# An offset for each step's key in a planner: the same steps in another order, in a linear attention with a two-layer FFN on one Trainium2 core

## The chip, the cores and the metric

The kernel runs on one core of a Trainium2 chip. The metric is device time in microseconds (us) of one execution: 371.3 us in the median of three runs of the kernel before (371.17 to 372.02). The engines are TensorE (PE, whose weight loads are shown apart as PEld), VectorE (DVE), ScalarE (ACT), GpSimd (POOL) and SyncE (SP); 16 DMA engines move data. All three runs agree within 0.3%.

## The reference

`q`, `k` and `v` have 8 batches of 8 heads with 576 tokens of 64 numbers. The attention has no softmax over pairs of tokens: each token gets 256 features, and a head's 576 keys are summed up in one 256 x 64 matrix. Behind it stands a feed-forward network (FFN) over all 4608 tokens, in which the heads of a token lie side by side as 512 numbers.

```
def phi(x):
    proj = np.einsum('bhsd,df->bhsf', x, w_phi)                  # 64 -> 128
    proj = proj - np.max(np.abs(proj), axis=-1, keepdims=True)
    return np.concatenate([np.exp(proj), np.exp(-proj)], axis=-1)
q_p, k_p = (phi(q), phi(k))
kv = np.einsum('bhsf,bhsd->bhfd', k_p, v)
z = np.sum(k_p, axis=2)
num = np.einsum('bhsf,bhfd->bhsd', q_p, kv)
den = np.einsum('bhsf,bhf->bhs', q_p, z)[..., None] + 1e-06
attn = num / den
...
h = np.maximum(x @ w_in, 0.0)          # 4608 x 512 by 512 x 2048
out = h * h @ w_out                    # 2048 -> 512
```

## The kernel before

**Steps.** The kernel doesn't issue instructions as it goes. It first records *steps* (`Op`), each a few instructions on one engine, then lets a planner put them in an order, and then emits them in that order. The recording passes over the batches (loads, `k_batch`, `q_batch`) and then over the FFN's chunks of tokens (`hp_chunk`, `op_chunk`). These are the steps, with the lines that the profile shows:

- Loads of `k`, `q`, `v` by POOL's DMA queue (L379 for 512 tokens of each head, L387 for the other 64, called "rest"); `w_in` in two halves (L406) and `w_out` in two halves (L411), all to bf16. One batch's `q`, `k` and `v` have two buffers each.
- Transposes of `k` and `q`: on PE for batches 0 and 1 (L508, L686, with an identity), by a transposing DMA of SP's queue from batch 2 on (L436, L440).
- Key features: `kp` (L537) projects, in five groups for each batch, with matmuls that use 64 rows of PE's array; DVE takes the largest absolute value (L475), ACT the two exponentials (L482), and `em` (L562) the exponentials of the largest values. The factors that belong to the subtraction of the maximum are multiplied to `v` (`va`, L604 and L594, on POOL, for batch 0 on POOL or DVE).
- `kv` (L621, L626): PE sums keys by values, with a column for `z`; ACT or DVE copies the result (L449, L451).
- Query features: `qm` (L708) and `qp` (L717), again on 64 rows, with a DVE maximum (L745) and two ACT exponentials (L739) and `e2` (L753).
- `nd` (L769; L777 for the rest tokens, where it uses 64 columns of the array): numerator and denominator; DVE adds the two halves (L797, L801), takes the reciprocal (L818) and multiplies (L825), which gives `xo`, 128 tokens of FFN input.
- The transpose of `xo` to `xT`: on PE for batches 0 and 1 (L860), by SP's DMA from batch 2 on (L844, L847).
- FFN, first product `hp` (L899): four chunks of 128 tokens, then sixteen of 256. Each chunk of 256 has eight hp steps of 8 matmuls with 256 columns; a chunk of 128 has four of 16 matmuls with 128 columns. ACT or DVE takes the ReLU (L914, L916), DVE squares it (L923).
- FFN, second product `op` (L945): for 128 tokens four steps of 4 matmuls with 512 columns, with the same PSUM buffer; then a copy (L449, L451) and a store by SP's queue (L969, L966).

**Buffers.** PSUM has two rings: `pj`, three buffers, for everything of the attention, and `mo`, two buffers, for the transposes on PE and for hp and op. A step that needs a buffer waits until the step that reads the last owner is done. Other rings are in SBUF: five for `xT`, two for the squared `h`, four for the ReLU's result.

**Keys and order.** Each step is recorded by `add` with a key, in microseconds: roughly when it is due. An FFN step's key comes from a list with a pitch of 1.2 us, in which hp steps of one chunk alternate with op steps of the chunk before. A step of the attention has a key some microseconds ahead of the chunk that will need it. `order` simulates the engines with fixed costs for each step. In each round it takes the engine whose earliest possible step starts soonest, and among the steps that can start there within a short window (`WINDOW`, 0.15 us on PE, 0.1 on ACT and DVE) it takes the one with the smallest key plus a penalty for starting later:

```
near = [c for c in can if c[2] == e0 and c[0] <= soon + self.WINDOW[e0]]
...
t, o, e = min(near, key=lambda c: c[1].key + self.BETA * (c[0] - soon))
```

Where a step may run on either of two engines, the planner takes the one on which it would be done sooner. The order that comes out, in time of the planner's simulation, is the order of every engine's instructions and of every DMA queue. Steps are numbered in the order of their recording; a DMA takes two numbers, one for its issue and one for its transfer.

Of the kernel before, what the change touches and what calls it, by code (L numbers as in the profile page):

```python
# [11 lines left out]
ALU = mybir.AluOpType  # L12
ACT = mybir.ActivationFunctionType
INF = float("inf")


class Slots:
# [8 lines left out]
    def take(self):  # L26
        n = self.free.index(min(self.free))
        self.free[n] = INF
        return n
# [48 lines left out]
class Plan:  # L78
# [21 lines left out]
        return o, d  # L100

    def add(self, key, engines, emit=None, deps=(), take=(), give=(), after=(), locks=(), port=False, mode="full"):
        op = Op(key, engines, emit, deps, take, give, after, locks, port, mode)
        self.ops.append(op)
        return op

    def order(self):
# [8 lines left out]
        def start(o, e):  # L116
# [12 lines left out]
            if o.ring:  # L129
                ring = rings.setdefault(o.ring[0], [])  # L130
                for n in range(len(ring) - self.DEPTH, len(ring) - self.DEPTH + o.ring[1]):
                    if n >= 0:
                        t = max(t, ring[n].seen or INF)
            if o.port and e in ("dve", "pool"):
# [5 lines left out]
        while ready:  # L140
            can = [(start(o, e), o, e) for o in ready for e in o.engines]
            soon, _, e0 = min(can, key=lambda c: c[0])
            if soon == INF:
                raise RuntimeError("; ".join(sorted(f"{o.emit.__qualname__} {o.key:.1f}" for o in ready if o.emit)))
# [64 lines left out]
def kernel(  # L209
# [154 lines left out]

    o_wst, d_wst = plan.issue("hw", 2, -99, {"sp": (1.2, 1.2)}, c_wst, 0.1)
    o_var = add(-99, {"dve": (1.9, 1.9)}, c_var)
    o_w2 = add(-98, {"dve": (0.6, 0.7)}, c_w2, [d_wst], after=[o_var])
    o_ready = add(-200, {"pool": (1.2, 1.2)})
    srcs = {"k": k, "q": q, "v": v}
    tiles, loads = {}, {}  # L370
# [648 lines left out]
```

## Time and profile before

| | before |
|---|---|
| runs shown, median (lowest to highest) | 371.3 us (371.17 to 372.02) |
| profiled execution | 370.85 us |
| its span, first to last instruction | 369.0 us |
| granted TensorE clock, mean | 0.998 |
| idle before the first transposes on PE, for k and for q | 6.6 us, 4.1 us |
| first hp matmul (L899) starts | 30.3 us |
| last op matmuls (L945) end | 365.0 us |

The profile is of one execution. Busy time is the time in which an engine had an instruction under way; a matmul's end is modelled, so that a busy PE may still lose time between matmuls. In the lists of waits a row gives the engine and line that waited, what it waited for, the sum in us, how often, and the longest. "Issue" there means that the profile shows nothing that the engine waited for. In the chain that ended last a row gives start, length and what ran.

The chain of the whole program is PE for 70% (L899 28%, L945 27%), then DVE 9% and DMA 8%. Loads fill the start: w_in's halves land at 22.1 and 27.7 us, batch 1's keys at 30.1, w_out's at 35.6 and 40.6, and the DMA engines are busy in nearly all of the first 110 us.

### The profile page before, as it was taken

What the parts mean: (1) busy time and instruction counts of PE and PEld (TensorE: products, weight loads), DVE (VectorE), ACT (ScalarE), POOL (GpSimd) and SP (SyncE); (2) the same over time, 40 slices, a digit from 0 to 9 for tenths busy, and PEclk for the clock granted to TensorE, in tenths of its full rate; (3) what the DMA queues carried; (4) which work ended last, traced back from release to release, by engine and by line L of the source; (5) the groups of instructions that cost most, each with busy time, mean ns of one, the idle gap of its engine ahead of it and who ended that gap; (6) DMA issues with size and microseconds to landing.
All of it is one profiled execution on the core that took longest, in us unless ns stands there. A gap on an engine that the chain in (4) does not pass through costs nothing.

```text
span 369.0 us, 9166 instructions
## 1 busy us (share of the span) xinstructions
PE 338.3 (92%) x3788; PEld 235.5 (64%) x3836; DVE 271.0 (73%) x463; ACT 239.6 (65%) x376; POOL 139.3 (38%) x181
## 2 busy tenths in 40 slices
PE   2378989899999999999899999999999999999995
PEld 2267756766686667477576756676677666767662
DVE  4979787999777678878756899679469896857220
ACT  2855677869577864477854898379648954654441
POOL 8644138966930069302390029200920191000000
PEclk9999999999999999999999999999999999999999
DMA  7999999999994272974918154762113102211112
GB/s 83 182 207 204 200 204 152 172 200 180 120 187 75 58 157 42 177 121 94 157 45 117 50 122 66 106 125 74 25 45 62 44 2 60 71 45 47 40 38 78
DMA packets 90009, 39.07 MB, mean 106 GB/s; under 512 B 57584, under 2 KB 84336, under 8 KB 89968
## 3 DMA queue, kind: packets, MB, share of 16 engines
q0 software_dynamic: 41168, 18.36, 40.2%
q1 hardware_dynamic: 48800, 20.13, 26.6%
q8 instruction: 30, 0.49, 0.5%
q14 instruction: 11, 0.09, 0.1%
HBM read 36.77 MB, written 9.44 MB: 125 GB/s over the span
## 4 chain that ended last, share of the span: by engine, by line
PE 70%; DVE 9%; DMA 8%; ACT 4%; issue 3%; POOL 3%; SPq 2%; DVEq 0%; ACTq 0%; POOLq 0%
PE mo L899 28%; PE mo L945 27%; DMA xT<-xo 5%; PE pj L626 4%; PE pj L769 3%; DVE m L475 3%; DMA vin<-in_v_dram 2%; ACT kph L482 2%; PE pj L708 2%; DVE h L923 2%; PE pj L717 1%; SPq L847 1%; PE pj L621 1%; PE pj L537 1%; DVE hr L916 1%
## 5 line engine op out<-in xcount | busy, mean ns | idle before, releaser
L899 PE MATMUL mo<-xT,win 128*128 128x256 bf16 (+1 forms) x1280 | 144.1, 262 | 3.5 <-DMA xT<-xo 1.9
L945 PE MATMUL mo<-wout,h 128*128 128x512 bf16 x528 | 135.4, 379 | 4.1 <-issue 1.0
L899 PEld LDWEIGHTS <-win 128*128 128x128 bf16 x1280 | 111.7, 98 | 31.3 <-issue 6.3
L914 ACT ACTIVATE hr<-mo 128x512 bf16<-128x512 f32 x113 | 67.7, 601 | 60.0 <-PE mo L899 55.9
L923 DVE TENSOR_TENSOR h<-hr 128x512 bf16<-128x512 bf16 x144 | 71.9, 509 | 34.3 <-ACT hr L914 33.9
L945 PEld LDWEIGHTS <-h 128*128 128x128 bf16 x576 | 52.9, 98 | 48.4 <-issue 2.6
L739 ACT ACTIVATE qph<-pj 128x1024 bf16<-128x1024 f32 (+1 forms) x80 | 71.6, 945 | 16.5 <-PE pj L717 16.3
L482 ACT ACTIVATE kph<-pj 128x1024 bf16<-128x1024 f32 (+1 forms) x80 | 71.2, 954 | 10.8 <-PE pj L537 7.6
L604 POOL TENSOR_TENSOR va<-vin,em 128x512 bf16<-128x512 bf16 x57 | 61.4, 1111 | 0.6
L745 DVE TENSOR_REDUCE mq<-pj 128x8 f32<-128x1024 f32 (+1 forms) x40 | 44.4, 1109 | 10.9 <-PE pj L708 10.1
L475 DVE TENSOR_REDUCE m<-pj 128x8 f32<-128x1024 f32 (+1 forms) x40 | 43.8, 1108 | 2.4 <-PE pj L537 2.2
L573 POOL CAST va<-em 128x64 bf16<-128x64 f32 (+1 forms) x11 | 4.9, 446 | 104.5 <-ACT em L562 104.5
L797 DVE TENSOR_TENSOR tmp<-pj,e 128x520 f32<-128x520 f32 x32 | 22.1, 691 | 15.4 <-PE pj L769 14.8
L825 DVE TENSOR_TENSOR xo<-tmp,rden 128x512 bf16<-128x512 f32 (+1 forms) x40 | 29.4, 736 | 0.3
L449 ACT ACTIVATE ot<-mo 128x512 f32<-128x512 f32 x30 | 18.0, 599 | 17.2 <-PE mo L945 13.4
L801 DVE TENSOR_TENSOR tmp<-pj,tmp 128x520 f32<-128x520 f32 x32 | 22.2, 695 | 6.1 <-PE pj L769 5.8
L769 PEld LDWEIGHTS <-qph 128*128 128x128 bf16 x512 | 20.6, 98 | 5.5 <-issue 1.0
L916 DVE TENSOR_SCALAR hr<-mo 128x512 bf16<-128x512 f32 x31 | 21.0, 683 | 3.8 <-PE mo L899 3.7
L626 PE MATMUL pj<-va,kph 128*128 128x65 bf16 x512 | 23.4, 200 | 0.0
L626 PEld LDWEIGHTS <-kph 128*128 128x128 bf16 x512 | 22.3, 102 | 1.1
L769 PE MATMUL pj<-kvs,qph 128*128 128x65 bf16 x512 | 22.4, 194 | 0.4 <-ACT kvs L449 0.4
L449 ACT ACTIVATE kvs<-pj 128x520 bf16<-128x520 f32 x15 | 9.1, 604 | 15.1 <-PE pj L626 15.1
(55 smaller groups left out, 244.4 us busy)
## 6 DMA issues: line engine op xcount, KB each, us to landing
out_dram<-ot SPq DMA_DIRECT2D x32, 256.0 KB, 2.4
vin<-in_v_dram POOLq DMA_DIRECT2D x8, 512.0 KB, 9.7
qin<-in_q_dram POOLq DMA_DIRECT2D x8, 512.0 KB, 9.2
kin<-in_k_dram POOLq DMA_DIRECT2D x7, 512.0 KB, 11.7
win<-in_moe_w_in_dram POOLq DMA_DIRECT2D x2, 1024.0 KB, 14.9
wout<-in_moe_w_out_dram POOLq DMA_DIRECT2D x2, 1024.0 KB, 19.3
out_dram<-ot SPq DMA_DIRECT2D x8, 128.0 KB, 2.3
xT<-xo SPq DMA_TRANSPOSE x36, 2.6
```

Source lines behind the costliest of these rows:

```text
L475: nc.vector.tensor_reduce(out=st["m"].rearrange("p (n c) -> p c n", c=2)[:, :, n0 : n0 + n], in_=st["pj", g][:, :, :n], axis=AX.X, op=ALU. ...
L482: nc.scalar.activation(out=st["kph"][:, s, n0 : n0 + n].rearrange("p n c f -> p c n f"), in_=st["pj", g][:, :, :n], func=ACT.Exp, scale=1. ...
L604: eng.tensor_tensor(out=st["va"][:, s, gs, 0:D], in0=tiles["v", b].rearrange("p h i d -> p (h i) d")[:, gs, :], in1=st["em"][:, s, gs].uns ...
L626: nc.tensor.matmul(out=kv[:, sum_of(h), :], lhsT=st["kph"][:, s, 2 * h + i // 2, i % 2, :], rhs=st["va"][:, s, h * NI + i, :], start=False ...
L739: nc.scalar.activation(out=st["qph", pt][:, s, :, n0 : n0 + n], in_=st["pq", pt, gi][:, :, :n], func=ACT.Exp, scale=1.0 - 2.0 * s)
L745: nc.vector.tensor_reduce(out=st["mq", pt][:, :, n0 : n0 + n], in_=st["pm", pt, gi][:, :, :n], axis=AX.X, op=ALU.max, apply_absolute_value ...
L769: nc.tensor.matmul(out=nps[:, sl, :], lhsT=qph[:, s, half, sl, :], rhs=kvs[:, s, sum_of(sl), :], start=True, stop=True)
L825: nc.vector.tensor_tensor(out=xo[:, :nh], in0=st["tmp", pt, half][:, :nh, 0:D], in1=st["rden", pt, half][:, :nh].unsqueeze(2).to_broadcast ...
L899: nc.tensor.matmul(out=hp[:, mi, :], lhsT=win[:, kc, mc * P : (mc + 1) * P], rhs=st_x[c][:, kc, 0:nt, :], start=(kc == 0), stop=(kc == KC1 ...
L914: nc.scalar.activation(out=out_, in_=in_, func=ACT.Relu)
L923: eng.tensor_tensor(out=st["h2"][:, mcs[0] : mcs[-1] + 1, 0 : nt * P], in0=hr, in1=hr, op=ALU.mult)
L945: nc.tensor.matmul(out=st["op"].rearrange("p a b -> p (a b)"), lhsT=hst["h2"][:, mc, tt * P : (tt + 1) * P], rhs=wout[:, mc, :], start=(mc ...
```

## The change

A table `SHIFT` has one whole number for each step in the order of recording, from -50 to 50; `add` adds half of it, so at most 25 us, to the step's key. Nothing else differs: the same steps are recorded with the same costs, buffers, engines to choose from and dependencies, and the planner is the same. The numbers were found by a search that ran without a chip. Since keys decide the order, and the order decides where a step with two possible engines goes, the order of instructions changes on all engines and on both DMA queues, and so does the engine of a few steps.

```
+SHIFT = (
+    -13, 0, -23, 5, -19, -5, 0, -11, 26, 0, -13, 0, -5, 0, -28, 0, -5, 0, -10, 0, -3, 0, -37, 0, 0, 0,
...
+    -2, 0, 4, -26, -17, -4, 0, 18, 0,
+)
...
     def add(self, key, engines, emit=None, deps=(), take=(), give=(), after=(), locks=(), port=False, mode="full"):
+        key += 0.5 * SHIFT[len(self.ops)]
         op = Op(key, engines, emit, deps, take, give, after, locks, port, mode)
```

## The prediction

> **What bounds the kernel now.** First the page's busy shares and the windows of 18.45 us: they show where TensorE, the busiest engine, loses time.
>
> ```profile
> PE 338.3 (92%) x3788; PEld 235.5 (64%) x3836; DVE 271.0 (73%) x463; ACT 239.6 (65%) x376; POOL 139.3 (38%) x181
> ...
> 0.00:18.45 18.45, 5.88 (x62) 4.22 (x62) 13.28 (x20) 10.80 (x19) 13.87 (x25) 1.00 1.04 132
> 18.45:36.90 18.45, 14.85 (x241) 12.72 (x243) 15.22 (x26) 10.49 (x17) 8.28 (x13) 1.00 1.25 206
> 36.90:55.35 18.45, 16.27 (x216) 11.98 (x219) 14.73 (x26) 13.17 (x21) 4.68 (x8) 1.00 1.46 202
> 55.35:73.80 18.45, 16.61 (x282) 12.47 (x285) 15.61 (x29) 14.43 (x24) 17.31 (x23) 1.00 1.30 162
> 73.80:92.25 18.45, 17.33 (x189) 11.60 (x187) 18.40 (x32) 14.96 (x24) 11.80 (x17) 1.00 1.51 190
> ...
> 239.85:258.30 18.45, 18.24 (x193) 12.63 (x194) 15.84 (x25) 15.72 (x24) 0.00 (x0) 1.00 0.47 100
> ```
>
> A row gives the stretch, then busy time of PE, PEld, DVE, ACT and POOL, then clock and DMA. From about 110 us PE is busy 98-99% of a window; before that it is not, and DVE is what is full (18.40 of 18.45). So there are two stages with two limits.
>
> To see what PE really loses I price its steps by their fastest rows in the chain of waits:
>
> ```profile
> 355.51 0.86 PE mo L945 x4
> 356.38 0.87 PE mo L899 x8
> ```
>
> With these and the like (one 8-matmul step at L769 0.24, one kv step at L621/L626 1.34) PE's whole program is 321.8 us of work. Following the trace's weight loads in program order, the step that comes after PE's 35th us of it starts at 62.1 us, after the 60th at 92.4, after the 85th at 118.1. Lost by then (start less the work done): 26.8, 31.6, 33.1. The last step stands at 43 lost. So 33 is gone by 118 us, only 10 after.
>
> The early part is DVE's. In program order, by waits direct and through other engines, I count how much DVE work must be finished before PE may start a step (DVE instructions priced by their group rows). "Lead" is that less the PE work already done: before PE's 35th us 10.9, its 60th 15.3, its 85th 10.8. DVE's idle time, from the windows, adds up to 5.2, 8.4, 12.1, 15.0, 15.0 at the ends of the first five. At 92 us lead plus idle is 15.3 + 15.0 = 30.3 against 31.6 lost; at 74 us (PE work 45) 12.7 + 15.0 = 27.7 against 28.7. That sum, plus about 1.2 us of latency, is what PE has lost: DVE sets the end of this stage.
>
> The late part: what PE and its weight loads wait for from 110 to 365 us.
>
> ```profile
> PEld L708 <- issue: 7.2, 21, 0.4
> PEld L899 <- issue: 3.9, 18, 0.3
> PEld L537 <- issue: 2.7, 9, 0.4
> PEld L777 <- issue: 1.7, 6, 0.4
> PEld L945 <- issue: 1.5, 7, 0.3
> ...
> PE mo L899 <- DMA xT<-xo: 1.9, 3, 0.9
> PE mo L945 <- issue: 0.6, 4, 0.2
> PE mo L899 <- ACT hr L914: 0.3, 1, 0.3
> ```
>
> PE waits for almost nothing (2.8 us). But weight loads stand idle, with no releaser, where a step on half of the array (L537, L708, 64 rows; L777, 64 columns) follows a whole-array step, and where a whole-array step follows it.
>
> **The change, part by part.** It removes no work: TensorE has the same matmuls, the same DMAs are issued. Three ReLU evictions go from DVE (0.683) to ACT (0.601), two kvs copies go from ACT and one va product from POOL to DVE, ten small copies swap between DVE and ACT: by the group rows DVE's sum rises by 1.1 us, ACT's falls by 1.0, POOL's by 1.1, none on the late path. What changes is the order, on every engine. PE's neighbours of different kind fall from 405 to 334: hp steps and op steps (the two FFN products) now stand in longer runs.
>
> 1. *Start.* The load queue of POOL keeps k0, v0, q0, w_in, k1, w_out, q1; only k2 goes ahead of v1. The first FFN step stands after 8.4 instead of 7.8 us of PE work and needs 21.4 instead of 21.0 us of DVE work; a transpose of k1 now stands just before it, and k1 landed at 30.1, the old first step began at 30.30. Nothing changes that DVE doesn't hide: 0.
>
> 2. *DVE's stage.* The new order asks more of DVE sooner: lead 15.3 at PE's 15th us (before 10.4), 17.0 at the 35th (10.9), 14.0 at the 60th (15.3), 15.3 at the 85th (10.8). More backlog should leave DVE less idle. These are its waits from 20 to 95 us before:
>
> ```profile
> DVE tmp L797 <- PE pj L769: 2.4, 1, 2.4
> DVE hr L916 <- PE mo L899: 1.9, 2, 1.1
> DVE m L475 <- PE pj L537: 1.6, 1, 1.6
> ```
>
> All are for PE steps that the order may bring sooner. Idle until 36.9 us (8.4) is the loads' and stays. Of the 6.6 us after it, I let half go, being unable to see more without a run: 11.7. PE has then lost 17.0 + 11.7 + 1.2 = 29.9 at its 35th us (more than the 26.8 of before) and, as the lead doesn't rise again, still 29.9 at its 85th, against 33.1: -3.2. Bounds: all 6.6 gone, 26.6, -6.5; none gone, 33.2, +0.1.
>
> 3. *Changes of array form.* After 80 us of PE work the order had 40 entries into half-array steps and 36 returns from 64-row steps; now 34 and 29. By the rows an entry costs (7.2 + 2.7 + 1.7) / 36 = 0.32, a return (3.9 + 1.5) / 25 = 0.22; spread over all 40 and 36, 0.29 and 0.15. So 6 x 0.29 + 7 x 0.15 = -2.8; at the full row price -3.4; if weight loads catch up inside the next step, 0. PE is full there, so I take -2.8.
>
> 4. *Other PE waits late.* 0.9 us besides DMA; covers between a step and the eviction it needs are longer in the new order (more PE work stands between). -0.5, from -0.9 to +0.5.
>
> 5. *Transposes by DMA* (L844, L847), which bring the FFN's input. PE work between the last PE step that a chunk's transposes need and the chunk's first step (its last one) was, in order of chunks, 8.5, 7.4, 9.2, 7.5, 8.0, 6.4, 8.3 up to PE's 185th us; now 6.6, 8.6, 6.4, 6.8, 7.4, 9.8, 6.6. The chain and the tile's view price it:
>
> ```profile
> 107.25 6.97 DMA xT<-xo
> ...
> 150.24 6.77 DMA xT<-xo
> ...
> DMA to landing us min/median/max: 2.3/2.6/7.7
> ```
>
> A clean landing takes 2.4; while q, v and k of a later batch are in flight (issued 98.7 to 106.0 and 144.1 to 152.8) it took 7. With 2.3 of DVE (0.69 + 0.70 + 0.20 + 0.74) and 1.2 of issue, clean is 5.9, inside every cover; met by loads 10.5, 3.8 beyond a cover of 6.7. The first load burst stands behind batch 2's products of V, which now wait for 67.1 us of DVE work (71.1 before), and the transpose that met it for 92.2 (89.8): 6.4 us further apart, against 7.7 of overlap. The next burst starts 6 us of PE work sooner. One may meet, one that met is freed: 0, from -1.9 (the waits above gone) to +3.8 (one more met).
>
> 6. *DVE beside POOL.* L923 takes 0.424 in the median and up to 1.259; in 55.3 to 92.2 us, thirteen took 7.98, 2.4 more than thirteen medians. Which of them stand beside POOL's products the order doesn't tell: 0, from -2.4 to +2.4. (The Trainium skill, SBUF — State Buffer, Who interferes with whom: a DVE instruction with two SBUF inputs and a GpSimd one that reads SBUF block each other for a whole instruction. The long ones agree. It speaks against a DVE that has less idle time while POOL works: by it the meetings would double, +2.4 in the sum, 367.2.)
>
> The last step, its copy and store stay: 32 matmuls of L945 at the end in the new order too.
>
> **Sum.** -3.2 - 2.8 - 0.5 = -6.5. The profiled execution took 370.85 us (span 369.0, 1.85 around it), so 364.35; the median of the runs is 0.45 above it: 364.8.
>
> **Rivals.**
> *DVE's stage gives nothing.* Idle stays 15.0, as its waits are for latency and not for backlog; for it: lead 17.0 comes as early as the 35th us. Against: more released work stands in front of DVE. -2.8 - 0.5: 368.0.
> *DVE never idles after the loads.* For it: lead never below 13.6 from PE's 10th to its 50th us. Against: three of its waits are for PE steps behind 2 us of chain. -6.5 - 3.4 - 0.5 - 0.5 (half of the DMA waits and more): 360.4.
> *Transposes meet loads (slower).* Place: the first step of the chunks with covers of 6.4 to 6.9 (five of them, three before). Price 3.8 each. It decides from two on: 7.6 - 6.5, 372.4; three, 376.2. For it: nine of the first twelve transposes of L844 and L847 took over 5 us to land. Against: the distances of part 5.
> *The order changes and the end doesn't*: each gain is eaten by a wait behind it, as PE is 92% busy: 371.
>
> **Chances.** Forecast 0.50, DVE gives nothing 0.18, DVE never idles 0.15, transposes 0.12, no change 0.05. A measurement of this kernel can tell 0.3%, 1.1 us. The first three are faster: 0.82 (0.01 of the second falls in the band); same 0.06; slower 0.12. The forecast's own range is 362 to 367; for 8 in 10 I take 359.0 (near the second rival with 1.4 below it) to 372.6 (two transposes met).
>
> **What would show it.** Right: DVE's busy time is near full from 37 us on, PE's loss at its 85th us near 30, weight loads' idle "issue" rows after 110 us down by about 3, PE's wait for xT under 3. Wrong: DVE idle of 15 us again by 75 us; PE waiting 4 us or more for xT after 100 us; L923 above 0.51 in the mean. If the gain comes from the first 30 us instead, part 1 is wrong.

## The result and the profile after

The changed kernel takes 376.82 us in the median (375.88 to 377.56, four runs) beside 371.51 for the kernel before (371.17 to 372.02): a ratio of 1.014, 95% interval 1.0114 to 1.0167. It was forecast at 364.8; it is slower, and the forecast missed by 12.0 us. Lines of the changed kernel are those of the kernel before plus 70.

The windows of the profiled execution (375.88 us, span 374.1; columns as before: stretch, PE, PEld, DVE, ACT, POOL, clock, DMA):

```profile
36.90:55.35 18.45, 16.95 (x219) 12.01 (x220) 15.13 (x27) 13.76 (x22) 5.69 (x9) 1.00 1.47 181
55.35:73.80 18.45, 15.01 (x236) 10.73 (x234) 11.93 (x24) 13.54 (x21) 13.68 (x18) 0.91 1.09 131
73.80:92.25 18.45, 18.45 (x216) 13.02 (x213) 16.05 (x32) 13.91 (x23) 12.05 (x19) 1.00 1.54 184
...
129.15:147.60 18.45, 15.55 (x161) 9.96 (x159) 15.29 (x19) 9.41 (x19) 16.71 (x21) 0.98 0.77 134
147.60:166.05 18.45, 18.45 (x193) 11.61 (x192) 11.77 (x21) 11.30 (x16) 0.75 (x2) 0.93 0.58 90
```

PE is full in 73.80 to 92.25 (17.33 before). But two windows stand out: PE 15.01 at 55 to 74 us (16.61 before) and 15.55 at 129 to 148, and the granted clock, 1.00 in every window shown of before, is 0.91 and 0.93 in or right after them. What PE waited longest for, from 30 to 160 us:

```profile
PE pj L691 <- POOL var L664: 3.3, 1, 3.3
PE pj L787 <- DVE tmp L877: 2.9, 1, 2.9
PE mo L969 <- DMA xT<-xo: 1.5, 1, 1.5
```

PE's loss, measured as in the prediction (start of a step less the PE work done before it), puts sizes to these:

| PE work done, us | 35 | 40 | 60 | 85 | 105 | 110 | 150 | 300 |
|---|---|---|---|---|---|---|---|---|
| before | 26.3 | 27.4 | 31.2 | 32.9 | 33.5 | 33.5 | 37.2 | 42.2 |
| after | 27.0 | 32.3 | 32.9 | 36.3 | 36.7 | 41.5 | 42.9 | 47.3 |

(Before stands up to 0.5 below the prediction's 26.8, 31.6 and 33.1 for the 35th, 60th and 85th us: differences of that size say nothing.) Two steps stand out, 5.3 and 4.8 us (35 to 40, 105 to 110), and 1.5 for xT within 80 to 85. Without them the changed kernel would have lost 47.3 - 5.3 - 4.8 - 1.5 = 35.7, which is 6.5 below 42.2, as much as was forecast. But this only subtracts: it takes the kernel before to lose nothing at these places (it lost 1.1 from 35 to 40), and the rest of the order to be unmoved by the stalls. The last experiments measure the order without them.

**First stall, near 64 us.** The chain that ended last, around it (start, length, what ran):

```profile
42.92 0.88 POOL kin L449
...
43.88 20.68 DMA vrest<-in_v_dram
...
64.63 1.04 POOL var L664
```

The rest of batch 1's V takes 20.68 us to land. It now stands behind batch 3's K (L449 at 42.92), and the loads ahead of it are late too. The timeline of SP's queue shows what else came sooner, first before, then after (start, length of the issue):

```profile
51.03 5.18 SPq L436 DMA_TRANSPOSE kT<-kin  x1
```

```profile
45.26 5.72 SPq L506 DMA_TRANSPOSE kT<-kin  x1
```

This is batch 2's K, transposed by DMA as soon as it has landed: at 45.17 now, 50.93 before, since its load went ahead of batch 1's V. The transpose takes 14.84 us in the midst of the loads (11.85 before), and what is behind it slips: the rest of batch 1's Q lands by 54.31 (52.46), batch 2's Q at 58.27 (55.26). That the transpose is what delays them is read from these times; the runs below move the load and the transpose together.

**What an idle PE costs on top.** Windows of 1 us, same columns:

```profile
64.00:65.00 1.00, 0.00 (x0) 0.00 (x0) 1.00 (x2) 0.94 (x2) 0.37 (x1) 1.00 1.07 136
65.00:66.00 1.00, 0.00 (x0) 0.00 (x0) 0.18 (x1) 0.00 (x0) 0.93 (x2) 1.00 1.49 126
66.00:67.00 1.00, 0.17 (x5) 0.17 (x5) 0.00 (x0) 0.00 (x0) 1.00 (x2) 1.00 1.46 136
67.00:68.00 1.00, 1.00 (x34) 1.00 (x32) 0.00 (x0) 0.00 (x0) 1.00 (x2) 1.00 1.09 145
68.00:69.00 1.00, 1.00 (x12) 0.48 (x9) 0.58 (x2) 0.71 (x2) 0.94 (x1) 0.61 0.92 58
69.00:70.00 1.00, 1.00 (x3) 0.15 (x1) 0.84 (x1) 0.80 (x1) 1.00 (x2) 0.50 0.16 10
70.00:71.00 1.00, 1.00 (x11) 0.51 (x11) 0.00 (x0) 0.33 (x1) 1.00 (x2) 0.50 0.00 0
71.00:72.00 1.00, 1.00 (x6) 0.42 (x5) 0.00 (x0) 1.00 (x2) 1.00 (x3) 0.69 0.33 66
```

PE stands still for 3.31 us from 63.52. Some 1.4 us after it starts again the clock is 0.50 for about 3.4 us: 0.39 + 0.50 + 0.50 + 0.31 = 1.70 us lost. So the step of 5.3 is 3.3 of waiting, 1.7 of half clock and small change. The second stall has the same form: 2.90 us idle, then 1.71.

**Second stall, near 143 us.** The squaring's row in the view of tile h (count, then shortest/median/longest in ns), before and after:

```profile
L923 DVE TENSOR_TENSOR h<-hr x144: 373/424/1259, 32.0 to 357.9; 128x512 bf16<-128x512 bf16 x144
```

```profile
L993 DVE TENSOR_TENSOR h<-hr x144: 375/418/6029, 34.3 to 356.9; 128x512 bf16<-128x512 bf16 x144
```

One squaring of 144 took 6.03 us, from 137.15 to 143.18. POOL's timeline beside it:

```profile
133.64 2.04 POOL L674 TENSOR_TENSOR va<-vin,em 128x512 bf16<-128x512 bf16 x2
135.63 0.96 POOL L449 DMA_DIRECT2D kin<-in_k_dram  x1
136.58 1.25 POOL L457 DMA_DIRECT2D krest<-in_k_dram  x2
137.84 6.24 POOL L674 TENSOR_TENSOR va<-vin,em 128x512 bf16<-128x512 bf16 x6
```

POOL ran six products of V one after the other, five of them at an undisturbed 1.05 to 1.08 us, while DVE got through part of one instruction. Before, the same eight products ran without a load between them, and DVE's and POOL's instructions took turns (mostly 1.26 and 1.22 us each). Behind the shut-out squaring stood L874 and L877, which free the PSUM buffer that PE's next qp step waited for.

### The profile page after: what moved, and what is told of

Same layout as the page of the kernel before. It is cut to its first block, busy times and chain, and to the rows that moved or that the text cites. A ratio compares the mean times of both kernels' runs of the same rounds, so it can differ in the third digit from the quotient of the medians.

```text
span 374.1 us, 9185 instructions
## 1 busy us (share of the span) xinstructions
PE 343.0 (92%) x3836; PEld 236.9 (63%) x3836; DVE 275.3 (74%) x465; ACT 240.1 (64%) x375; POOL 140.5 (38%) x180
## 4 chain that ended last, share of the span: by engine, by line
PE 66%; DMA 12%; DVE 11%; POOL 6%; issue 3%; ACT 0%; DVEq 0%; POOLq 0%; ACTq 0%
PE mo L969 26%; PE mo L1015 26%; DMA vrest<-in_v_dram 6%; DVE h L993 5%; PE pj L696 4%; PE pj L839 3%; POOL va L674 3%; DMA kin<-in_k_dram 2%; DMA vin<-in_v_dram 2%; PE pj L778 2%; DMA xT<-xo 2%; PE pj L607 2%; DVE mq L815 1%; PE pj L787 1%; POOL krest L457 1%
## 5 line engine op out<-in xcount | busy, mean ns | idle before, releaser
L969 PE MATMUL mo<-xT,win 128*128 128x256 bf16 (+1 forms) x1280 | 139.0, 262 | 1.7 <-DMA xT<-xo 1.5
L1015 PE MATMUL mo<-wout,h 128*128 128x512 bf16 x576 | 138.2, 384 | 0.1
L969 PEld LDWEIGHTS <-win 128*128 128x128 bf16 x1280 | 112.1, 98 | 23.8 <-issue 3.7
L984 ACT ACTIVATE hr<-mo 128x512 bf16<-128x512 f32 x116 | 69.3, 598 | 47.1 <-PE mo L969 41.1
L993 DVE TENSOR_TENSOR h<-hr 128x512 bf16<-128x512 bf16 x144 | 77.2, 550 | 23.9 <-ACT hr L984 23.4
L664 POOL TENSOR_TENSOR var<-vrest,em 64x512 bf16<-64x512 bf16 x14 | 15.0, 1073 | 50.3 <-PE mo L969 25.8
L895 DVE TENSOR_TENSOR xo<-tmp,rden 128x512 bf16<-128x512 f32 (+1 forms) x40 | 28.5, 719 | 0.4
L986 DVE TENSOR_SCALAR hr<-mo 128x512 bf16<-128x512 f32 x28 | 19.0, 684 | 9.6 <-PE mo L969 9.5
```

Source lines behind the costliest of these rows:

```text
L895: nc.vector.tensor_tensor(out=xo[:, :nh], in0=st["tmp", pt, half][:, :nh, 0:D], in1=st["rden", pt, half][:, :nh].unsqueeze(2).to_broadcast ...
L969: nc.tensor.matmul(out=hp[:, mi, :], lhsT=win[:, kc, mc * P : (mc + 1) * P], rhs=st_x[c][:, kc, 0:nt, :], start=(kc == 0), stop=(kc == KC1 ...
L984: nc.scalar.activation(out=out_, in_=in_, func=ACT.Relu)
L993: eng.tensor_tensor(out=st["h2"][:, mcs[0] : mcs[-1] + 1, 0 : nt * P], in0=hr, in1=hr, op=ALU.mult)
L1015: nc.tensor.matmul(out=st["op"].rearrange("p a b -> p (a b)"), lhsT=hst["h2"][:, mc, tt * P : (tt + 1) * P], rhs=wout[:, mc, :], start=(mc ...
```

## The experiments

In all but one of them the planner's finished order is edited and the rest stays. The edits are shown as changes of an engine's queue: k2 is the load of batch 2's K, "rest v1" that of the 64 rest tokens of batch 1's V, kT2 the transpose of K. Each run's kernel has line numbers of its own, so the text says which step a line is. "Loss" is PE's loss at that many us of its work.

**Each stall by itself (1).** In the changed kernel the rest of V goes ahead of batch 3's K:

```diff
 POOL  q2
+POOL  rest v1
 POOL  k3
-POOL  rest v1
```

> The changed kernel with one DMA issue moved in POOL's queue: the 64 rest tokens of batch 1's v are loaded ahead of batch 3's k, as in the kernel before, not behind it. Theory A (the loss of 5.2 us between PE's 35th and 40th us is this load, which landed at 64.6 us while POOL stood ready for it at 60.0): the rest load lands about 4 us sooner, POOL's wait at L664 (4.6 us) falls below 1, kv's wait for var (3.3 us) goes, and the time falls by 3 to 5 us, from 376.8 to 372 to 374. Rival B (VectorE bounds this stage, lead 17.0 in the prediction, and would have stopped PE anyway): under 1 us. Rival C (POOL is late because it issues six DMAs between its products): POOL's wait goes but kv still waits 2 us or more; 1 to 2 us.

Measured 377.82 us (377.45 to 378.03), ratio 1.0154 (1.0116 to 1.0192). The wait for V is gone, but PE now waits 3.1 us for the rest of batch 1's Q at 52.8 us (the half clock that it brings lasts 6.83 us), and its loss at 40 is still 31.1. So the place of V's rest behind batch 3's K isn't the cause by itself: the loads ahead of it are late as well. A new stall came at 98 us: PE waits 3.9 us for batch 2's products, which stand in POOL's queue behind a load that waits.

**Each stall by itself (2).** DVE's first sum of the denominators (L874, L877) goes ahead of the squaring that was shut out:

```diff
+DVE   L874, L877 of tile pair 2
 DVE   squaring (6.03 us)
-DVE   L874, L877 of tile pair 2
```

> The changed kernel with one VectorE step moved: at 137 us the sum of the rest tokens' numerator (L874, L877) goes ahead of three squarings of chunk 7, of which the first took 6.03 us in the changed kernel while POOL made six products in a row. Theory A (PE lost 5 us between its 100th and 110th us because qp waited for the PSUM buffer that this sum frees, behind the squaring): qp's wait of 2.9 us goes, a part of it comes back at the op step that needs the squares; 1.5 to 4 us faster, 373 to 375.5. Rival B (op steps need the squares at the same moment): under 1 us.

Measured 373.17 us (372.16 to 377.17, ten runs), ratio 1.0050 (1.0016 to 1.0085): some 3.5 us less than the changed kernel. A squaring is still shut out, 5.18 us, but nothing urgent stands behind it, and the loss from 105 to 110 is 1.2 instead of 4.8. The profiled execution (376.21) shows the stall at 97 us too, 6.6 us of waiting and 6.83 of half clock; seven of the ten runs, at 372.2 to 373.9, are faster than that.

This profile shows something more. Up to 135 us the changed kernel, this run and the next one give every engine and queue the same instructions in the same order. Yet PE's first long wait is 3.3 us for V's rest near 64 us in the first, and 3.0 and 2.4 us for Q's rest near 53 us in the other two, and the stall at 97 us, 6.6 and 5.1 us, is not in the first at all. So where a stall of this order falls differs from one execution to the next. One profile shows what can happen, and a change of the median needs all runs.

**Each stall by itself (3).** The same stall from POOL's side: the load of k7 and its rest go behind batch 3's products.

```diff
 POOL  va, va
-POOL  k7, rest k7
 POOL  va x6
+POOL  k7, rest k7
```

> The changed kernel with three DMA issues moved: the loads of batch 7's k and its rest go behind POOL's last product of batch 3 and no longer stand between its second and third. Theory A (the squaring was shut out for six products because it began to wait while POOL wrote DMA descriptors, and POOL then never left a gap): no squaring takes over 1.3 us there, four in a row take about 5 us and not 8.7, qp's wait falls by 3 or more, and the time by 2 to 4 us. Theory A2 (POOL's products in a row shut VectorE out whatever stands before them): a squaring of 4 us or more remains, at most 1 us gained. Nothing else needs batch 7's k before PE's 149th us, so that its later load costs nothing by either.

Measured 376.46 us (375.04 to 378.11), ratio 1.0133 (1.0081 to 1.0185). No DVE instruction is over 1.6 us, and the loss from 105 to 110 is 0.1: the load between the products goes with the shut-out. The time isn't won: the median is 0.4 us below the changed kernel's, a miss. The profiled execution loses 5.07 us to batch 2's products at 97 us, but that is ahead of the moved load, so the edit can't have made it. The other three runs are slower than the profiled one and at a lower clock (0.982 to 0.985 beside 0.994); what they wait for isn't recorded.

**Late steps alone.** The offset is used only where a step's key is 130 or more.

```diff
-        key += 0.5 * SHIFT[len(self.ops)]
+        key += 0.5 * SHIFT[len(self.ops)] if key >= 130.0 else 0.0
```

> The kernel before, with the table's offsets on steps whose own key is 130 or more alone (about PE's 115th us of work and after). In the changed kernel PE lost 5.9 us after its 110th us of work, before 9.2. Theory A (fewer changes of array form late are a gain of their own): 2.5 to 3.5 us faster than before, 368 to 369, and fewer idle weight loads by issue after 130 us. Rival B (the late gain is only slack that the early stalls gave, as VectorE and the loads had got ahead): within 1 us of before.

Measured 378.13 us (377.79 to 378.47), ratio 1.0163 (1.0125 to 1.0201). Early it is the kernel before (loss at 110: 34.6 beside 33.5), but from 150 to 170 it loses 5.3 where both others lose 0.4 to 1.1: DVE falls behind, and from 110 us on PE waits 2.6 us for squarings and its weight loads 5.0. Neither expectation came. Two halves of two orders make a third one with a hole at the seam; it says nothing of the late order's worth.

**The load order (1).** In the changed kernel one load is put back:

```diff
 POOL  q1
+POOL  v1
 POOL  k2
-POOL  v1
```

> The changed kernel, with one load of POOL's queue put back: batch 1's V ahead of batch 2's K. Theory A (the order of the loads): in the changed kernel batch 2's K lands at 45.2 us instead of 50.9, so its transpose by DMA starts at 45.3 instead of 51.0, takes 14.8 us and slows the loads that stand behind it; put back, the transpose starts near 51, the rest of Q of batch 1 lands by 52.5 (54.3), and the wait that PE has before its 40th us shrinks: loss there about 29 to 30 instead of 32.3, median 373 to 375. Theory B (the new order of the products and squarings wants its operands too soon, whatever the loads do): loss at the 40th us stays near 32, median 376 to 377.5.

Loss at 40 is 26.8, below before's 27.4, with no half clock there: the first stall is gone entirely, and theory B with it. That was more than expected, but the median is only 376.13 (373.37 to 378.66), ratio 1.0114 (1.0076 to 1.0152). In the profile the sum of keys by values (L729) waits for batch 2's products, and qp (L820) behind the shut-out squaring:

```profile
PE pj L729 <- POOL va L706: 5.2, 1, 5.2
PE pj L820 <- DVE tmp L910: 2.9, 1, 2.9
```

These are PE's longest waits from 60 to 160 us: the stall at 94 us, which the three edits above had at 97 to 98 us, and the shut-out squaring (6.04 us).

**The load order (2).** The reverse, in the kernel before:

```diff
 POOL  q1
-POOL  v1
 POOL  k2
+POOL  v1
```

> The kernel before, with one load moved as the change moves it: batch 2's K ahead of batch 1's V, nothing else. Theory A: its transpose starts 5 us sooner, among the loads, the rest of batch 1's Q and V land 2 to 3 us later, and PE loses 1 to 5 us by its 50th us: 373 to 377. Theory B: no change, 371 to 372.5.

375.23 us (373.46 to 377.77), ratio 1.0094 (1.0064 to 1.0125): the one move costs the kernel before 3.5 us by that ratio. The transpose of K starts at 45.36 and takes 14.53, batch 2's Q lands at 60.02, and PE's loss at 40 is 30.8 (27.4). The profile shows 1.26 and 1.71 us of idle close together, then 3.41 us of half clock. All profiles of this case agree on this move, though their stalls differ: by the measure of the table, loss at 40 is about 30 to 32.5 in the five kernels with batch 2's K ahead of batch 1's V, and about 27 to 29.5 in the ten with it behind.

**The load order (3).** Three loads put back, the transposes as they come out of that.

```diff
 POOL  q1
+POOL  v1
 POOL  k2
-POOL  v1
...
+POOL  rest v1
 POOL  k3
-POOL  rest v1
+POOL  rest k2
 POOL  va of batch 1
-POOL  rest k2
```

> The changed kernel with three loads put back: batch 1's V ahead of batch 2's K, the rest of batch 1's V ahead of batch 3's K, and the rest of batch 2's K ahead of batch 1's products of V. Theory A: no wait of 3 us before PE's 40th us, so no half clock after it either: loss there 27.5 to 28.5 (before 27.4, changed 32.3); the transpose of batch 3's K starts before 69 us and not at 71.1, ahead of the next burst of loads. The squaring of 6 us near 137 stays with its 5 us. Median 371 to 372.5. Theory B: 375 to 377.5.

A miss: 378.20 us (376.85 to 381.41), ratio 1.0175 (1.0095 to 1.0255). Loss at 40 is 28.2, as expected, but there are now three stalls of 2.9 to 4.1 us, each with 3.41 us of half clock: for kT at 75 us, for xT at 117, and the squaring at 146.

**Both stalls removed.** The run above, with L874 and L877 ahead of the squaring as well.

```diff
+DVE   L874, L877 of tile pair 2
 DVE   squaring
-DVE   L874, L877 of tile pair 2
```

> The run above, and DVE's first sum of the denominators' step of tile pair 2 ahead of the squaring that took 6.03 us. If the two stalls (before PE's 40th us, before its 110th) are all that the changed kernel loses against the forecast, each as a wait of about 3.3 us and 1.7 us of half clock behind it: loss at the 110th us 31 to 32.5, no half clock after 20 us, median 366 to 368. If the stalls only move (another wait takes the place of each), 371 to 375.

373.30 us (371.71 to 376.57), ratio 1.0044 (1.0011 to 1.0077): "the stalls only move". The chain that ended last names the next one:

```profile
67.65 1.17 SPq L541
...
68.91 7.71 DMA kT<-krest
...
76.67 0.39 PE pj L640 x3
```

On SP's queue (L541) the transpose of the rest of K stands behind that of the rest of Q (67.65) and so comes at 68.91, when the next loads start (68.50): 7.71 us, and PE (kp, L640) waits for it. At 110.40 the first xT meets loads in the same way: 7.28 us.

**Transposes of K first.** The run above, with SP's order of before at that place:

```diff
 SP    qT2
+SP    rest kT2, kT3
 SP    rest qT2
-SP    rest kT2
-SP    kT3
```

> The run with three loads put back and the sum ahead of the squaring, and on SP's queue the transposes of batch 2's last rows of K and of batch 3's K ahead of the transpose of batch 2's last rows of Q, as before the change. Theory C (each stall left is a transpose by DMA that runs while loads are in flight): the transpose that was issued at 68.9 and took 7.7 us starts by 64 and lands by 69, so the wait of 2.6 us near 75 us and its 1.7 us of half clock go: loss at PE's 50th us 27.5 to 28.5 instead of 32.0, median 368 to 369.5 (373.3 less 4.5). If another wait takes its place: 372 to 374.

370.26 us (368.26 to 371.92), ratio 0.9958 (0.9927 to 0.9988): the stall at 75 us is gone (loss at 50: 27.5, expected 27.5 to 28.5), and the kernel is faster than before for the first time, by less than expected. What is left is 3.17 us for xT at 112 us and its half clock.

**Loads out of xT's way.** Twice, with batch 6's K in the place of batch 7's, and that one behind the products of V, then behind the last load of Q:

```diff
 POOL  q5, v4, rest v4, rest q5
-POOL  k6, rest k6
 POOL  va, va (batch 3)
-POOL  k7, rest k7
+POOL  k6, rest k6
 POOL  va x6
+POOL  k7, rest k7
```

> The run above, with the load of batch 6's K (issued at 106.6, landed at 116.9) moved behind the second of batch 3's products of V and the load of batch 7's K behind the last of them, so that the first transposes of the FFN's input near 110 us meet fewer loads. Theory C: that transpose lands in 3 to 5 us instead of 7.3, PE does not wait 2.6 us near 115 us, and no half clock follows: median 364 to 366, which is what the prediction said of the order. If it only moves the stall: 367 to 371.

370.04 us (367.53 to 371.66), ratio 0.9943 (0.9913 to 0.9974). The stall at 112 is gone (loss at 110: 32.3), but xT of the next chunk, issued at 147, takes 7.4 us beside k7, and that costs 4.4.

```diff
-POOL  k7, rest k7
 POOL  q6, v5, rest v5, rest q6, q7, rest q7
+POOL  k7, rest k7
```

> The run before last's kernel (batch 6's K moved to the place of batch 7's K), with batch 7's K moved further, behind the last load of Q, at about 176 us; it is transposed at about 216. In the run with it directly behind the products of V, the transposes of the FFN's input issued at 146 to 147 took 7.3 to 7.4 us amid the loads, PE waited and a half clock of 1.7 us followed: 4.4 us by PE's 120th us of work. Theory C: with 0.5 MB less in flight there these transposes land 2 us sooner, no wait of 3 us is left, no half clock after 20 us; loss at PE's 120th us 31.5 to 33 (before 33.7, changed 41.8), median 365 to 367.5, faster than the kernel before by 1.0 to 1.6%. If a stall moves on: 369 to 371, as in the last two.

372.18 us (370.23 to 375.18), ratio 1.0018 (0.9991 to 1.0046): no difference that can be told. Loss at 140 is 33.3 (35.6 before), then k7 meets the transposes at 173 us, which take 8.4; PE waits 4.3 and the half clock follows. A stall moved on twice, for one load of 0.5 MB.

**No stall left.** k7 goes behind batch 6's V, at 187 us, where no transpose of xT is near:

```diff
-POOL  k7, rest k7
 POOL  va of batch 4, v6, rest v6
+POOL  k7, rest k7
```

> As the run before, but batch 7's K goes behind batch 6's V, at about 187 us, where the trace shows no transpose of the FFN's input between 175 and 203 us; its own transpose is due at about 216. Theory C: the transposes issued at 173 to 175 us, which took 8.4 us beside that load, land in 4 to 5 as in the run with K of batch 7 in the products, the wait of 4.3 us and its half clock go: loss at PE's 150th us 33.5 to 35 instead of 39.5 (before 37.2), at its end 37 to 39 (before 42.1), profiled span 364.5 to 366.5, median 366 to 368.5 (the runs of the last two varied by 3 to 5 us). If a stall moves on again: 369 to 372.

367.50 us (366.55 to 367.80), ratio 0.9885 (0.986 to 0.991): faster than both kernels; its slowest run is below the fastest of before beside it (370.69). These are windows of its profile, and PE's waits from 40 to 365 us, whole:

```profile
0.00:18.45 18.45, 5.83 (x62) 4.11 (x62) 12.77 (x20) 10.20 (x18) 14.65 (x26) 1.00 1.10 142
18.45:36.90 18.45, 15.24 (x241) 12.93 (x242) 15.31 (x28) 11.42 (x19) 5.98 (x11) 1.00 1.26 206
36.90:55.35 18.45, 18.22 (x252) 13.09 (x250) 16.19 (x30) 15.07 (x26) 6.42 (x11) 1.00 1.47 194
55.35:73.80 18.45, 16.25 (x279) 12.42 (x277) 17.02 (x29) 13.91 (x20) 14.67 (x18) 1.00 1.28 147
73.80:92.25 18.45, 18.27 (x186) 12.30 (x184) 15.68 (x31) 12.71 (x21) 14.97 (x21) 1.00 1.53 190
...
129.15:147.60 18.45, 17.49 (x213) 11.01 (x212) 16.10 (x23) 9.03 (x15) 13.46 (x16) 1.00 1.01 138
```

```profile
PE pj L736 <- DVE mq L860: 1.7, 2, 1.0
PE mo L976 <- DVE xo L941: 1.1, 1, 1.1
PE pj L649 <- DMA kT<-kin: 0.9, 1, 0.9
PE pj L741 <- POOL va L718: 0.6, 1, 0.6
PE mo L1063 <- DVE hr L1032: 0.2, 1, 0.2
```

(L736 and L741 are kv, L976 is the transpose of xo on PE, L649 kp, L1063 op.) No idle stretch of PE after 30 us is over 1.12 us until its work ends, and the clock is 1.00 until then. Loss is 28.1 at 40, 30.6 at 85, 32.1 at 110 and 37.9 at 300.

**The shut-out by itself.** In the kernel before, only batch 7's K is moved between the second and the third product:

```diff
 POOL  va, va
+POOL  k7, rest k7
 POOL  va x6, q6, v5, rest v5, rest q6
-POOL  k7, rest k7
```

> The kernel before, with one load moved as the change moves it: batch 7's K between the second and the third of batch 3's products of V on POOL. Theory D (a DVE instruction with two inputs in SBUF that begins to wait while POOL writes a transfer's descriptors is shut out until POOL's run of products ends): one squaring or product of DVE near 140 us takes 4 to 6 us (longest before 1.5); PE loses 0 to 5 us there, 371 to 376. If the length of that instruction in the changed kernel came of DVE's own new order: none over 1.6 us, 371 to 372.

```profile
L957 DVE TENSOR_TENSOR h<-hr x144: 376/422/6589, 31.6 to 359.7; 128x512 bf16<-128x512 bf16 x144
```

One squaring of 6.59 us in the old order, where the longest was 1.26: the load between the products brings the shut-out, and DVE's new order isn't needed for it. Nothing urgent stood behind it there, so the loss from 85 to 110 grows by only 1.5 us, where it grew by 0.6; 373.14 us (372.55 to 376.59), ratio 1.0042 (1.0014 to 1.0071).

## Why the prediction was wrong

*1. Start, costed at 0.* This step failed. It named the move ("only k2 goes ahead of v1") and looked at who waits for the loads' data, not at what a landed load sets off: the transpose by DMA 5.8 us sooner, amid the loads. It also left out the rest of V behind batch 3's K, as it ended its list of POOL's queue at q1. The move alone costs 3.5 us in the kernel before; taken back, the first stall of 5.3 is gone from the profile, though other stalls kept that run's median at 376.13.

*2. DVE's stage, -3.2.* Near in size where no stall covers it, borne out only in part as a mechanism. Loss at PE's 85th us was forecast at 29.9; the stall-free run has 30.6, the changed kernel 36.3 - 5.3 - 1.5 = 29.5. DVE's idle time up to 73.8 us was forecast at 11.7: 12.5 in the stall-free run (by its four windows), and 18.9 in the changed kernel, where the first stall leaves DVE empty. The sign that was named for "wrong", 15 us by 75 us, thus came, for another reason than the rivals'. But the forecast needs 11.7 to hold up to PE's 85th us of work, and the stall-free run's idle time is 15.3 at 92.25 us, beside 15.0 before. DVE's idle time came later there and isn't less, so what carries the gain up to PE's 85th us stays open.

*3 and 4. Array forms and other late waits, -3.3 together.* Nearly right. From 110 to 300 us of PE work the kernel before lost 8.7, the changed one 5.8: -2.9. The stall-free run loses 5.8 there too (37.9 - 32.1), so this gain isn't slack that the stalls gave. The prediction's "busy 98-99% of a window" from 110 us on was misread, as two windows of before show 95% and 94%:

```profile
147.60:166.05 18.45, 17.56 (x163) 11.70 (x164) 14.14 (x25) 11.46 (x17) 2.92 (x5) 1.00 1.14 149
166.05:184.50 18.45, 17.36 (x176) 11.47 (x179) 14.71 (x24) 14.58 (x22) 5.61 (x9) 1.00 0.81 126
```

The weight loads' "issue" rows shown of before add up to 17.0; those of the changed kernel from 110 us on:

```profile
PEld L778 <- issue: 7.4, 23, 0.4
...
PEld L969 <- issue: 2.3, 10, 0.3
PEld L1015 <- issue: 2.0, 8, 0.3
PEld L607 <- issue: 1.8, 7, 0.4
PEld L847 <- issue: 1.6, 6, 0.4
```

15.1, so 1.9 of the 2.8. It comes from L969 (3.9 before, as L899) and L607 (2.7, as L537); L778 (7.2, as L708) gave nothing.

*5. Transposes by DMA, 0, from -1.9 to +3.8.* For xT it held: one wait of 1.5. But the step, and the rival built on it, counted xT alone (L844, L847). The transposes of K and Q on the same queue (L436, L440) meet the same loads, earlier and for longer, 14.84 us. The rival "transposes meet loads" was right as a mechanism, given a chance of 0.12 and tied to the wrong place. That its figure for three met, 376.2, lies near the measured 376.82 is luck: only one wait for xT came.

*6. DVE beside POOL, 0, from -2.4 to +2.4.* The other failed step: both its bounds came from meetings of one product each (1.26 us at most). One meeting with six products cost 4.8 by itself (2.9 of waiting, 1.7 of half clock). The rule cited there from the Trainium skill (SBUF — State Buffer, Who interferes with whom: the ports that the two engines share are an exclusive lock) was priced at one instruction each, +2.4; the trace shows a block that lasted into the sixth instruction in a row.

*Left out altogether.* A wait of PE of about 3 us was priced at its length. The two of the changed kernel brought 1.7 us of half clock each: 3.4 us of its time, and part of what the next stall in each experiment cost.

In sum: forecast 364.8, plus 5.3, 4.8 and 1.5 makes 376.4, beside 376.82 measured. That this comes out so closely is partly luck, as the order without stalls is worth less than forecast: the stall-free run shows 4.0 us (371.5 to 367.5), not 6.5. By PE's 85th us it is -2.3 for -3.2 (32.9 to 30.6), from there to its 300th -2.0 for -3.3 (9.3 to 7.3). Of what is missing, up to 1.2 is the squaring that is still shut out in that run (loss 30.9 to 32.1 from 105 to 110); the rest stays open. These 4.0 us belong to the new order with its loads and a few steps placed by hand. The kernel before with batch 6's and 7's K placed as late was not run, so what the places of the loads are worth by themselves stays open too.

## What to carry to other kernels

A list of what a reorder moves has to hold the loads together with what their landing sets off: a load that comes sooner may start a transpose by DMA among the loads that others wait for. Where a plan's costs are fixed numbers, its order can be good and its time bad: here most gaps that were closed let another one open, often a transfer that now met loads, until the last load was put where the trace showed nothing beside it. And a wait of TensorE near 3 us should be priced at its length plus the half clock that comes with it, up to 1.7 us here, so that one wait of 3 us costs more than three of 1. Where executions differ as they do here, a stall should be laid to a step only when several profiles or the medians agree.

## What the runs showed of the hardware

*Idle PE and the clock.* Over the 15 profiles, every stretch of 2.58 us or more in which PE did nothing (17, between 40 us and the end of its work) came with about 3.4 us at a granted clock of 0.50, three of them with twice that: 1.70 to 1.71 us less of full clock, or 3.41 to 3.42. In the changed kernel it began 1.4 and 1.1 us after PE's work resumed; in nine of the 17 it began while PE still stood, by up to 2.8 us, and that part cost nothing more. Of the shorter stretches over 1 us, only those of 1.79 and 1.94, and the pair of 1.26 and 1.71 in the kernel before with one load moved, brought it too; one of 2.41 did not. The Trainium skill (TensorE: Matmul & The Clock Gate, HAM oscillation — how this bites in real kernels) puts the limit at idle gaps over about 3.4 us and explains it by a window of that length. The length of the half clock agrees with it; the limit is lower here.

*DVE shut out by POOL.* In all eleven kernels in which a load stood behind the second of batch 3's eight products, one squaring took 5.17 to 6.59 us while POOL ran the next five or six products, most of them at 1.05 to 1.09 us. In the four in which that burst had no load inside it (the kernel before, the same with batch 2's K moved, the late steps alone, the loads behind the products) no squaring was over 1.31 us. What decides between taking turns and being shut out isn't shown: the shut-out squaring began sometimes while POOL wrote descriptors (137.15, 139.29) and sometimes just after a product had begun (132.26 against 132.08).
